# The first batch of a fused attention and FFN kernel: other first loads, scales written by ScalarE, and a new issue order

## The chip, the cores and the metric

The kernel runs on one core of a Trainium2 chip. The time is the device time of one execution in microseconds (us). A result is the median of several executions. Ratios are the mean time of one kernel's fast runs over that of the kernel before in the same rounds on the same chip, so they are not quite the ratio of the medians that are quoted beside them. A span is the length of one profiled execution; it is about 1.8 us shorter than that execution's time.

Engines: PE is TensorE (PEld its weight loads), DVE is VectorE, ACT is ScalarE, POOL is GpSimd, SP is SyncE. A name with a q (SPq, ACTq) is the engine's instruction queue, seen when it issues a DMA.

## The reference, cut to what matters

```python
# q, k, v: 8 batches x 8 heads x 576 rows x 64;  w_phi: 64 x 128
def phi(x):
    proj = einsum('bhsd,df->bhsf', x, w_phi)
    proj = proj - max(abs(proj), axis=-1, keepdims=True)
    return concatenate([exp(proj), exp(-proj)], axis=-1)
kv  = einsum('bhsf,bhsd->bhfd', phi(k), v);   z   = sum(phi(k), axis=2)
num = einsum('bhsf,bhfd->bhsd', phi(q), kv);  den = einsum('bhsf,bhf->bhs', phi(q), z) + 1e-6
x = (num / den) as 4608 rows x 512
out = (max(x @ w_gate, 0) * (x @ w_val)) @ w_out        # 512 -> 1536 -> 512
```

Each batch's x feeds the FFN. TensorE has most to do in the FFN, and that can't start before the first batch's attention has given its first x. The time until then is the ramp.

## The kernel before

All work is cut into some 850 pieces, and a list of numbers, `ORDER` ("the list" below), gives the order in which they are emitted. Every engine then runs its own instructions strictly in that order. A token `44:6` is piece 44 in PSUM bank 6 (or the pair 6 and 7); `z14:2` stands for 14 units of dummy matmul on zeros, which are meant to keep TensorE's clock up where the model expected it to be idle. The loads are pieces too: 1 is wv0 (a third of w_val), 2 wg0, 10 wg2 (the last third of w_gate), 12 wo0, 15 qm0 (tail rows of q, two small DMAs), 16 k2 (k of batch 2), 17 kt2 (tail rows of k, four small DMAs); 6 is wg1 and 13 wo1. A batch's tail is its last 64 rows of 576; late k is k of heads 4 to 7 of batch 0. A value scaling multiplies v by the scales (`scale_v` below), a kv product is a matmul of phi(k) with scaled v, an xu is the finished x of one chunk of 128 rows, and a k piece is k of two heads.

```python
def scale_v(dst, src, ek):                 # v times exp of the row maxima, on GpSimd
    nc.gpsimd.tensor_tensor(dst[:, :, :, 0:D], src ..., ek ..., op=ALU.mult)
    nc.gpsimd.tensor_copy(dst[:, :, :, D], ek)          # the scale itself, for z
# the row's normaliser: x = u * r, also on GpSimd, then transposed by TensorE to feed the FFN
    nc.gpsimd.tensor_tensor(x["xu"], x["u"][:, :, 0:D], r.to_broadcast([P, 8, D]), op=ALU.mult)
def k_crosswise(st):                       # groups 0 and 1 of batch 0: maxima and exps by half
    for par in range(2):
        k_max(st, 4, slice(par, par + 1)); k_exps(st, 4, 0, slice(1 - par, 2 - par))
    k_scales(st, 4)
# ... the first loads:
nc.scalar.dma_start(out=wf[0:D], in_=w_phi)
nc.gpsimd.dma_start(out=w2[D:P], in_=w_phi)
for u in range(NU):                        # NU = 4 groups of two heads
    if u < 2:
        load_kqv(0, "kn", k, nc.sync, FP32, slice(2 * u, 2 * u + 2))     # k piece u
    load_v(0, 2 * u, 2 * u + 2, nc.scalar)
load_first_tail(0); load_tail(inputs["vt", 0], 0, 1, v, nc.sync)
make_identity(nc, ident[FP32]); nc.gpsimd.tensor_copy(ident[BF16], ident[FP32])
for u in range(2):
    nc.gpsimd.dma_start(out=late_k[...], in_=k[0, 4 + 2 * u : 6 + 2 * u, 0:SF, :] ...)
# ...
nc.scalar.copy(w2[0:D], wf[0:D])           # the w copy: the first projection needs it
```

Of the kernel before, what the change touches and what calls it, by code (L numbers as in the profile page):

```python
# [46 lines left out]
ORDER = """z22:0 43:76 48:5 44:6 45 z6:4 49:0 z14:2 53:5 0 50 z12:4 54:2 65:7 3 59:6 4 56 1 5 z9:4 66:4 46 67  # L47
68 60:0 61 62 51 55 z56:7 70:4 77 69 84:5 52:6 63 71:02 72 7 11 73 47:7 z9:4 102:6 108:5 114:4 64:2
103:0 9 78:63 104 57 80 8 2 97:5 17 58:2 79 109:3 110 10 74:52 98:6 75:2 111 99 81:52 15 z15:3 76:4
105 82:3 126:2 120:5 85:03 87 139:2 100 86 533:7 88:53 121:0 525:2 6 83:7 89 90 541:2 122 16 526:7  # L50
13 115:3 527:5 101 106 152 123 107:2 18 170 116 117 91:67 168 112 124 528:5 542:7 171 92:6 113:0
94:51 95:2 535:7 543:6 127:30 129 536:7 118 12 128 544:2 177 130:50 96:7 93:3 131 534:4 119:2 125:7
140:53 14 132 142 529:2 133:70 539:1 162 134:4 136:32 537:0 141 538:7 530:1 545:0 189 137:7 20 546:4
21 143:52 153 144 163:0 145 531:7 547:4 164 135:2 19 552:3 166 165 138:5 172:6 173 540:2 553 149:45
554 167 169 150:0 146:12 183 175 174 548:5 549:4 532:3 154:60 155 550 156 147:5 551 221 184:2 22
190:0 178:6 555:5 556 558:4 186 179 180 229 191 185 557 559 187 151:6 192 148:7 157:23 176:5 560
561:3 158:76 195 196:40 197 567:2 24 583:3 181 193 188:6 198 208 159:7 182:4 23 223 241 160:5 562:0
199:61 200 242:3 201 194:5 243 563:0 25 26 584:1 568:2 244 28 575:7 230:5 224:0 222 565:2 573:3 231
225 205:47 566:2 574:3 235 226 232 564:7 206:4 577:2 260 202:30 245 273 576:1 579:7 203:2 227 580:0
236:5 289 209:31 238 211 204 578:7 233 585:0 210 569:1 237 570:2 591:7 291 207 29 212:53 213 239  # L60
581:1 214 571:2 33 298 572:3 215:45 582:6 228:1 246:2 247 30 218:35 240:1 219:4 592 216:2 234:1 283
220 593 292 248:53 284:1 249 217 586 587 310 250 304 588:7 251:35 285 290 252 594:0 595 253 589 286
27 254:65 596 257:34 255:5 590 597:6 598:4 258:7 603:5 287 305:0 342 307 256 261:26 31 263 613:4 262
161 306 609:5 604:6 316 308 614:7 615:4 299:0 264:26 265 266 610:5 605:4 356 300 34 601:6 302 301
274 602:7 35 616:5 259 270:62 32 309:3 617:4 267:75 271:0 618:1 607:6 272 608:2 599:7 311:0 329
275:35 313 277 600:2 611:7 276 312 288 619:5 303:6 606:2 394 620:7 268:0 612:1 293:2 317:46 295
624:0 318 627:1 269 628 319 294 625 320:62 321 357:4 412 410 314 629 626 343 322 296 358 278:23 344
297:6 279:71 350 315:0 39 280:3 639:6 359 323:20 630:1 37 360 637:3 326:07 324:6 631 345:4 351:2 38
347 632 362 352 621:0 327:7 622 635:6 623 281:1 325 633:7 346 634:6 638:0 353 419 354 640:1 330:46
331 653:0 332 645:1 348 654:2 36 646:3 355:0 333:16 363:4 334 335 636:3 647:0 643:6 413 42 364  # L70
339:73 328 644:2 411 365 649:6 361:3 648:7 366 340:0 336:12 655:6 651:7 425 337:0 381 395 349:5 341
652:6 396:13 426:5 397 641:7 398 427 656:0 663:4 642:7 368 428 367:3 650:2 414:0 369:52 664 666:7
338 416 463 667 41 431 370 665 371 689:2 668 420:5 515 422 415 372:03 374 373 421 657:2 660:7 450
661 691:3 669:4 378:56 423 375:01 376:3 662 658 379:4 40 659 687:1 404 399:03 670:2 690:1 405:6
382:42 407 477 417 384 683:0 671:1 429 406 383 692:2 688:3 408 400:01 681:2 684:3 672:1 675:2 385:64
432:0 386 673:3 424:2 387 433 434 682:4 418:5 377 388:36 465 679:7 674:2 464 677:4 391:30 437 389:1
380 676:2 685:7 680:0 471 430:1 435 392:7 686:6 409 390 393 678:5 483 478:3 480 438:60 693:2 694 439
699:5 440 436:0 695 484:6 479 282 441:30 481 700 702:2 442 443 701 485 696:0 486 705:1 703 401:3
447:45 444:67 697 402:1 704 445:3 698 709:7 706:4 707:5 472:6 451:02 474 453 708:4 452 516 710:5
719:2 473 448:3 482:4 713:5 723:0 454:61 466:3 502 456 489 455 724:5 720:0 446 717:1 467 711:2 714:5  # L80
457:01 460:67 449 468 475 469 712:2 715:5 458:1 487 461:0 718:3 470:4 727:7 490:15 491 716:4 732:0
725:7 492 733 488:1 721:2 476:1 493:35 462 459 494 728:7 729:2 726:1 722:7 403 730 495 738:1 496:73
731 745:4 497:3 498 499:56 747:2 743:7 734 500:6 503:24 735:7 741:0 736 504 739 740 505 737 506:52
742:4 746:7 744:0 507 508 748:1 509:45 510:0 749:6 751:7 750:3 759:2 760:1 512:07 513:6 752:5 757:4
753:7 761:6 755:0 758:7 756:1 517:24 518 519 768:0 763:1 501 511 771:7 754:6 762:5 764:4 769 774:3
514 520:21 775 521:65 522:4 765:1 772 776 770 777:2 799:6 766 781:0 767 773 779:0 778:6 800:7 780:5
523:6 787:4 782:7 788:3 793:2 783:1 784:0 794:7 524 797:6 789:5 791:7 798:6 785:0 792:7 813:1 790:0
786:2 795:1 804:0 801:7 796:6 802 805 806 810:1 807:2 803 811 823:0 812 817:3 808 809 829:7 814:6
818:5 824:7 815:6 816:0 827:7 819:1 828:0 835:2 830:1 821:0 836:7 831:6 820:5 822:7 833:6 834:0
825:7 826:1 832:0 837:2 838 846:3 839 847:7 843:6 848:7 840:5 841 844 845 842"""  # L90
# [6 lines left out]
def kernel(  # L97
# [23 lines left out]
    P = 128  # L121
# [127 lines left out]
    def scale_v(dst, src, ek):  # L249

        nc.gpsimd.tensor_tensor(  # L251
            dst[:, :, :, 0:D],
            src[:, :, None, :].to_broadcast([P, *dst.shape[1:3], D]),
            ek[:, :, :, None].to_broadcast([P, *dst.shape[1:3], D]),
            op=ALU.mult,
        )
        nc.gpsimd.tensor_copy(dst[:, :, :, D], ek)  # L257
# [15 lines left out]
    def k_exps(st, n, at, pars=slice(0, 2)):  # L273

        if "kp" not in st:
            st["kp"] = st["pool"].tile([P, 2, 2, 4, F], BF16, name="kp")
        kp = st["kp"][:, :, :, at : at + n]
        for s, sign in ((0, 1.0), (1, -1.0)):
            nc.scalar.activation(kp[:, s, pars], st["rows"][:, pars], AF.Exp, scale=sign)  # L279

    def k_max(st, n, pars=slice(0, 2)):

        if "m" not in st:
            st["m"] = sb_s.tile([P, 8], FP32, name="mk")[:, 0 : 2 * n]
        m = st["m"].rearrange("p (j i) -> p i j", i=2)
        row_max(m[:, pars], st["rows"][:, pars])

    def k_scales(st, n):
        st["ek"] = sb_s.tile([P, 8, 2], FP32, name="ek", bufs=8)[:, 0 : 2 * n]
        for s, sign in ((0, -1.0), (1, 1.0)):  # L290
            nc.scalar.activation(st["ek"][:, :, s], st["m"], AF.Exp, scale=sign)  # L291

    def k_crosswise(st):

        for par in range(2):
            k_max(st, 4, slice(par, par + 1))
            k_exps(st, 4, 0, slice(1 - par, 2 - par))
        k_scales(st, 4)

    def k_values(st, b, u):  # L300
        vs = st["vs"] = sb_k.tile([P, 8, 2, E], BF16, name="vs")
        vn = inputs["vn", b][:, 2 * u : 2 * u + 2].rearrange("p h c d -> p (h c) d")
        scale_v(vs, vn, st["ek"])

    def k_values_tail(st, b, at):

        ekm = sb_s.tile([P, NU, 2, 2], FP32, name="ekm", bufs=2)
        nc.gpsimd.tensor_tensor(
            ekm,
            st["ek"][:, at : at + NU, :, None].to_broadcast([P, NU, 2, 2]),  # L310
            half[:, None, None, :].to_broadcast([P, NU, 2, 2]),
            op=ALU.mult,
        )
# [3 lines left out]
    def k_kv(st, b, u, copy):  # L317
# [21 lines left out]
        copy(kv.rearrange("p h s e -> p (h s e)"), pk[:, 0 : 4 * E])  # L339
# [265 lines left out]
    def k_pieces(rank, st, start, ops, needs, take, name, banks, late=(), n=4, at=0, wide=True):  # L605
# [12 lines left out]
        if wide:  # L618
            wide_pieces(rank, st, n, at)
# [4 lines left out]
            lambda: k_crosswise(st),  # L624
            [
                ("DVE", 0.6),
                ("ACT", 0.48, None),
                ("ACT", 0.48, None),
                ("DVE", 0.6, 2),
                ("ACT", 0.48, 0),  # L630
                ("ACT", 0.48, 0),
                ("ACT", 0.21, 3),
            ],
            [(rank, "proj")],
            (rank, "rows", 0),
            free=[((rank, "proj"), 5)],
        )

    def wide_pieces(rank, st, n, at, done=lambda: None):
        plan.add(  # L640
            rank,
            "kmax",
            lambda: (k_max(st, n), k_scales(st, n)),
            [("DVE", 0.1 + n * 0.287), ("ACT", 0.21)],
            [(rank, "proj")],
            (rank, "rows", 0),
# [499 lines left out]
```

## Time and profile before

| | before |
|---|---|
| time, median | 390.13 us |
| span of the profiled execution | 388.2 us |
| TensorE busy | 374.4 us, of which dummy matmuls 11.9 us |
| TensorE without dummies | 362.5 us (374.4 - 11.9) |
| first FFN matmul | 34.1 us |
| last idle of TensorE in the ramp ends | 41.7 us |

The table by stretches of the kernel before. After the stretch and its length: busy time (and instructions) of PE, PEld, DVE, ACT and POOL, then TensorE's granted clock, the busy share of the DMA engines (transfers overlap, so it can exceed 1), and GB/s.

```profile
0.00:10.00 10.00, 5.88 (x32) 2.74 (x32) 2.42 (x9) 2.94 (x6) 6.38 (x14) 0.89 0.91 205
10.00:20.00 10.00, 9.92 (x100) 5.73 (x98) 7.60 (x12) 8.76 (x23) 7.83 (x8) 0.94 1.31 207
20.00:30.00 10.00, 7.50 (x136) 5.99 (x134) 9.58 (x18) 6.42 (x15) 8.93 (x13) 0.91 1.25 249
30.00:40.00 10.00, 9.15 (x138) 7.24 (x137) 7.26 (x14) 8.56 (x17) 7.85 (x11) 0.92 1.42 189
40.00:45.00 5.00, 4.15 (x96) 4.03 (x94) 3.75 (x6) 4.43 (x11) 5.00 (x5) 1.00 1.34 189
45.00:50.00 5.00, 5.00 (x101) 4.58 (x97) 4.39 (x11) 3.77 (x8) 3.68 (x5) 1.00 1.43 149
```

TensorE has gaps in the first 42 us and none from 45 us on; the DMA engines are full all the time. Parts of the timeline matter (start, length, engine, line, operation, out<-in; in brackets the idle time before it and what ended that). First the start, on all engines:

```profile
5.61 0.66 PE L240 MATMUL pall<-ident,vn 128*128 128x128 f32 x4 [0.90 <-DMA vn<-in_k_dram]
...
7.84 0.30 ACT L1036 CAST w<-wf 64x128 bf16<-64x128 f32 x1 [5.61 <-DMA kt<-in_k_dram]
8.19 0.61 PE L265 MATMUL pall<-w,tT 64*128 64x128 bf16 x8 [1.93 <-ACT w L1036]
...
11.19 1.91 POOL L251 TENSOR_TENSOR vs<-vn,ek 128x1024 bf16<-128x1024 f32 x1 [3.63 <-ACT ek L291]
```

The second k piece comes at 5.6 us. The first projection waits for the w copy on ScalarE at 7.84 us, and the first value scaling on GpSimd starts at 11.19 us. Then GpSimd around 35 us:

```profile
32.25 0.68 POOL L172 DMA_DIRECT2D qm<-in_q_dram  x1 [1.24 <-DMA wv_sb<-in_moe_w_val_dram]
...
34.79 0.82 POOL L215 DMA_DIRECT2D wg_sb<-in_moe_w_gate_dram  x1 [0.62 <-DMA kt<-in_k_dram]
35.61 0.90 POOL L163 DMA_DIRECT2D kn<-in_k_dram  x1
36.49 0.77 POOL L222 DMA_DIRECT2D wo_sb<-in_moe_w_out_dram  x1
37.26 0.25 POOL L308 TENSOR_TENSOR ekm<-ek,half 128x16 f32<-128x16 f32 x1
```

GpSimd issues loads one after the other: wg1, k2 and wo1 (in this list wg2 came earlier), some of them after a wait for an earlier DMA, and only then starts on the second batch's tail (37.26 us). TensorE, at the end of the ramp:

```profile
39.81 1.07 PE L457 MATMUL pall<-xT,wv_sb 128*128 128x128 bf16 x16
41.73 0.65 PE L323 MATMUL pall<-vs,kp 128*128 128x65 bf16 x16 [0.85 <-POOL vs L257]
```

It waits 0.85 us for the second batch's value scaling. That wait is the last in the ramp.

### The profile page before, as it was taken

To read this page: it belongs to the slowest core of one execution; us is meant where nothing else is said; L and a number is where in the kernel's file an instruction comes from. 1 tells how busy PE (TensorE), PEld (TensorE's weight loads), DVE (VectorE), ACT (ScalarE), POOL (GpSimd) and SP (SyncE) were. 2 spreads that over 40 slices of the span, in tenths; PEclk is the share of its full clock that TensorE was granted. 3 is DMA by queue.
4 is the path that set the end of the run, shared out by engine and by line. 5 is a ranking of instruction groups with operands and counts; after the bars stand their busy time and mean duration, and the time that the engine had idled before them with its cause. 6 is when DMAs were issued, how large, how long until landed. Compare 5 with 4: busy or idle time off the path is not lost.

```text
span 388.2 us, 8993 instructions
## 1 busy us (share of the span) xinstructions
PE 374.4 (96%) x3611; PEld 209.2 (54%) x3611; DVE 239.7 (62%) x413; ACT 240.2 (62%) x479; POOL 157.1 (40%) x178
## 2 busy tenths in 40 slices
PE   5979999999999999999999999999999999999994
PEld 2557898665465454645545465555545454444452
DVE  2797898868866777776746876577437443322330
ACT  2968868898848868778675767586463513413311
POOL 6797855684770684564305526236021101000000
PEclk9998999999999999999999999999999999999999
DMA  8999998999999794999474332210222011002003
GB/s 205 207 250 188 188 223 118 177 209 220 161 121 165 180 180 78 184 227 162 54 138 79 112 70 69 86 25 2 41 81 71 14 43 66 14 29 81 1 15 95
DMA packets 92506, 44.94 MB, mean 116 GB/s; under 512 B 58352, under 2 KB 87984, under 8 KB 92464
## 3 DMA queue, kind: packets, MB, share of 16 engines
q1 hardware_dynamic: 62352, 28.98, 33.5%
q0 software_dynamic: 28464, 13.78, 27.8%
q10 hardware_dynamic: 1648, 1.61, 1.3%
q8 instruction: 28, 0.46, 0.5%
q14 instruction: 14, 0.11, 0.1%
HBM read 37.81 MB, written 9.44 MB: 122 GB/s over the span
## 4 chain that ended last, share of the span: by engine, by line
PE 87%; POOL 6%; issue 3%; DMA 3%; DVE 0%; ACT 0%; ACTq 0%; POOLq 0%; DVEq 0%
PE pall L457 48%; PE pall L483 23%; PE pall L402 5%; PE pall L265 4%; PE pall L323 4%; DMA kt<-in_k_dram 3%; PE pall L357 2%; POOL vs L251 2%; PE pall L331 1%; POOL vsm L251 1%; PE pall L510 1%; POOL wv_sb L215 0%; POOL wg_sb L215 0%; PE pall L429 0%; DVE h L470 0%
## 5 line engine op out<-in xcount | busy, mean ns | idle before, releaser
L470 DVE SCALAR_TENSOR_TENSOR h<-pall,val_sb 128x512 bf16<-128x512 f32 x108 | 73.8, 686 | 74.9 <-PE pall L457 67.2
L466 ACT CAST val_sb<-pall 128x512 bf16<-128x512 f32 x108 | 63.5, 596 | 59.5 <-PE pall L457 47.5
L483 PE MATMUL pall<-wo_sb,h 128*128 128x512 bf16 x420 | 99.9, 379 | 0.0
L457 PE MATMUL pall<-xT,wv_sb 128*128 128x512 bf16 (+1 forms) x528 | 95.1, 321 | 0.5 <-ACT val_sb L466 0.5
L457 PE MATMUL pall<-xT,wg_sb 128*128 128x512 bf16 (+1 forms) x528 | 94.0, 321 | 0.0
L419 POOL TENSOR_TENSOR xu<-u,r 128x512 bf16<-128x512 f32 x36 | 37.4, 1044 | 124.8 <-DVE r L417 86.6
L251 POOL TENSOR_TENSOR vs<-vn,ek 128x1024 bf16<-128x1024 f32 x32 | 61.0, 1907 | 37.5 <-ACT ek L291 32.6
L279 ACT ACTIVATE kp<-pall 128x1024 bf16<-128x1024 f32 (+1 forms) x78 | 70.4, 966 | 8.5 <-PE pall L265 7.7
L457 PEld LDWEIGHTS <-wv_sb 128*128 128x128 bf16 x576 | 47.0, 98 | 41.7 <-issue 0.6
L457 PEld LDWEIGHTS <-wg_sb 128*128 128x128 bf16 x576 | 46.7, 98 | 40.1
L483 PEld LDWEIGHTS <-h 128*128 128x128 bf16 x420 | 38.6, 98 | 42.0
L247 DVE TENSOR_REDUCE mq<-pall 128x8 f32<-128x1024 f32 x36 | 43.8, 1220 | 17.2 <-PE pall L265 13.6
L247 DVE TENSOR_REDUCE mk<-pall 128x8 f32<-128x1024 f32 (+1 forms) x39 | 43.8, 1133 | 5.3 <-PE pall L265 3.2
L493 ACT COPY out_sb<-pall 128x512 f32<-128x512 f32 x35 | 20.5, 589 | 40.6 <-PE pall L483 37.5
L411 DVE TENSOR_TENSOR t<-pall,cq 128x455 f32<-128x455 f32 (+3 forms) x80 | 33.5, 419 | 17.8 <-PE pall L402 14.1
L374 ACT ACTIVATE qp<-pall 128x512 bf16<-128x512 f32 x60 | 36.6, 610 | 3.2 <-PE pall L357 3.1
L414 DVE TENSOR_TENSOR u<-pall,t 128x455 f32<-128x455 f32 (+3 forms) x80 | 34.2, 428 | 6.5
L375 ACT ACTIVATE qp<-pall 128x512 bf16<-128x512 f32 x60 | 37.0, 617 | 0.0
L402 PEld LDWEIGHTS <-qp 128*128 128x128 bf16 x640 | 27.5, 98 | 11.6 <-issue 1.2
L402 PE MATMUL pall<-kv,qp 128*128 128x65 bf16 x640 | 29.9, 195 | 1.2 <-DVE u L414 0.9
L323 PE MATMUL pall<-vs,kp 128*128 128x65 bf16 x512 | 20.7, 193 | 1.0 <-POOL vs L257 0.9
L323 PEld LDWEIGHTS <-kp 128*128 128x128 bf16 x512 | 18.8, 97 | 4.5 <-issue 1.3
(69 smaller groups left out, 269.2 us busy)
## 6 DMA issues: line engine op xcount, KB each, us to landing
out_dram<-out_sb SPq DMA_DIRECT2D x32, 256.0 KB, 2.4
vn<-in_v_dram SPq DMA_DIRECT2D x7, 1024.0 KB, 6.8
qn<-in_q_dram POOLq DMA_DIRECT2D x8, 512.0 KB, 8.2
kn<-in_k_dram POOLq DMA_DIRECT2D x7, 512.0 KB, 8.5
wv_sb<-in_moe_w_val_dram POOLq DMA_DIRECT2D x3, 512.0 KB, 13.3
wg_sb<-in_moe_w_gate_dram POOLq DMA_DIRECT2D x3, 512.0 KB, 10.3
wo_sb<-in_moe_w_out_dram POOLq DMA_DIRECT2D x3, 512.0 KB, 10.5
vn<-in_v_dram ACTq DMA_DIRECT2D x4, 256.0 KB, 5.6
```

The lines of the kernel that those rows point to most:

```text
L247: nc.vector.tensor_reduce(m, banks, axis=AX.X, op=ALU.max, apply_absolute_value=True)
L251: nc.gpsimd.tensor_tensor(dst[:, :, :, 0:D], src[:, :, None, :].to_broadcast([P, *dst.shape[1:3], D]), ek[:, :, :, None].to_broadcast([P, ...
L279: nc.scalar.activation(kp[:, s, pars], st["rows"][:, pars], AF.Exp, scale=sign)
L323: nc.tensor.matmul(kv_ps[:, hh, s, :], lhsT=st["kp"][:, s, c % 2, 2 * hh + c // 2], rhs=st["vs"][:, 4 * hh + c, s, :], start=(hh == s == c ...
L374: nc.scalar.activation(x["qp"][:, s, a], cols[:, 0], AF.Exp, scale=sign)
L375: nc.scalar.activation(y["qp"][:, s, b], cols[:, 1], AF.Exp, scale=sign)
L402: nc.tensor.matmul(banks[s][:, i], lhsT=x["qp"][:, s, slot, P * blk : P * (blk + 1)], rhs=kvs[b, h // 2][:, h % 2, s, :],)
L419: nc.gpsimd.tensor_tensor(x["xu"], x["u"][:, :, 0:D], r.to_broadcast([P, 8, D]), op=ALU.mult)
L457: nc.tensor.matmul(ps[:, n * i : n * (i + 1)], lhsT=w[:, dc, P * fi : P * fi + P], rhs=xT[:, dc, lo:hi], start=(dc == 0), stop=(dc == NDC ...
L466: nc.scalar.copy(st["val", step], ps)
L470: nc.vector.scalar_tensor_tensor(st["h2"][:, fis[0] : fis[-1] + 1, lo:hi], ps.rearrange("p (a b) -> p a b", b=n), 0.0, st["val", step].rea ...
L483: nc.tensor.matmul(st["po", t], lhsT=st["h2"][:, fi, P * t : P * t + P], rhs=wo_sb[:, fi, :], start=(fi == 0), stop=(fi == NFC - 1),)
```

## The change

Its intent: shorten the chain that leads to the first x. ScalarE writes the scales into v's extra column by itself, so that GpSimd copies nothing; groups 0 and 1 of batch 0 are handled at full width, with the two signs of exp as separate pieces; w is loaded in two halves on two queues and copied in one piece; late k goes first on GpSimd, in one DMA, and GpSimd's other loads are held until the second k piece is in; and the whole list is ordered anew after a model of the issue times. Cut to its core:

```diff
-    def k_crosswise(st): ...
+    if "z" in st:                                        # in k_scales, batch 0
+        vs = st["vs"] = sb_k.tile([P, 8, 2, E], BF16, name="vs")
+        for s, sign in ((0, -1.0), (1, 1.0)):
+            nc.scalar.activation(vs[:, :, s, D], st["m"], AF.Exp, scale=sign)
+    def k_scales_halves(st):                             # first tail: masked by a bias of -1e30
+        ... nc.scalar.activation(st["ekm"][:, :, s, hh], st["m"], AF.Exp, scale=sign, bias=other[...])
-        copy(kv..., pk[...])                             # batch 0: VectorE
+        nc.scalar.copy(kv..., pk[...])
-    nc.scalar.dma_start(out=wf[0:D], in_=w_phi)
-    nc.gpsimd.dma_start(out=w2[D:P], in_=w_phi)
+    nc.gpsimd.dma_start(out=late_k, in_=k[0, 4:8, 0:SF, :] ...)
+    for u, eng in enumerate((nc.scalar, nc.sync)):
+        if u:
+            eng.dma_start(out=wf[D * u : D * (u + 1)], in_=w_phi)
+        load_kqv(0, "kn", k, nc.sync, FP32, slice(2 * u, 2 * u + 2))
+        if not u:
+            eng.dma_start(out=wf[D * u : D * (u + 1)], in_=w_phi)
+    for lo, hi in ((0, 2), (2, 4), (4, 8)):
+        load_v(0, lo, hi, nc.scalar)
+    held = singles.tile([P, 1], FP32)
+    nc.gpsimd.tensor_copy(held, inputs["kn", 0][:, 2, 0, 0:1])
-    nc.scalar.copy(w2[0:D], wf[0:D])
+    nc.scalar.copy(w2, wf)
-ORDER = ... 143 dummy units ...
+ORDER = ... 92 dummy units; wv0 and wg0 behind the value scalings of batch 0 ...
```

## The prediction

> **What bounds the kernel now.** From about 42 us on TensorE never waits: the table by stretches shows it busy 50.0 of 50 us in nearly every stretch from 50 to 350 us. Only the ramp is open. Before 42 us TensorE is busy 33.6 us, of which 11.9 us (group of L999, 39 matmuls) are dummy matmuls on zeros; so useful work is 21.7 us and 20.3 us are lost. All that the change can win lies there: once the FFN matmuls run without gaps (first at 34.1 us, no gap after 41.7 us), each us saved before is one of the end.
>
> **The chain in the ramp (timeline, waits).** The first k transposes are in SBUF at 5.3 us, but the first projection starts at 8.19 us: it waits for the w copy on ScalarE (7.84 us), which stands in program order behind five DMA issues, the last of them held back until 7.43 us. The first row maxima are then interleaved with half-wide exps, and GpSimd's first value scaling starts at 11.19 us. From there GpSimd is the chain: scalings of 1.91 us, each with a 0.25 us copy of the scales, a 0.22 us mask product, DMA issues between; the last ends at 24.3 us, the first numerator at 26.2 us, the first FFN matmul at 34.1 us.
>
> **Removed.** One of ScalarE's DMA issues ahead of the w copy; GpSimd's w load; about 1.5 us of copies and mask on GpSimd; weight and k1 issues between the scalings. **Added.** Per group two ScalarE exps of about 0.16 us, four small ones for the first tail, kv evacuations on ScalarE (0.39 us) instead of VectorE (0.42 us); one GpSimd op that holds the q load until the second k piece is in. **Moved.** Half of w to the SyncE queue, late k first on GpSimd, wv0/wg0 behind all four scalings, w copy early.
>
> **Sum.** I estimate the w copy at 4.5 to 6 us, projection at about 5.5, first maximum (1.22 us) and scales by 8.1: first scaling 3 us earlier. Then 1.5 us less on GpSimd and fewer issues between: the last scaling of the first batch ends near 19.5 to 20 us instead of 24.3. Not all of the 4.5 us reaches the end: DMA is full from 2 us to 60 us (slices), and wv0, issued near 20 us instead of 6 us, takes about 10 us to land (issue table: 13.3 us median), so the FFN starts near 29.5 to 31 us. The Trainium skill ("DMA: Bandwidth & Descriptors", section "Issuing engines are not separate DMA queues") says that all issuers share 16 engines, so using both queues saves issue time, not transfer time; the trace agrees (9 tenths busy while three queues run). As a second count, the dummy units in the order fall from 143 to 92; at 11.9/143 = 0.083 us that is 4.3 us, if the order's model is right. I take 3.7 us.
>
> **Prediction.** 386.5 us, range 383.3 to 389.6. Faster by over 2%: 0.06; within 2%: 0.92; slower: 0.02.
>
> **What would show it.** w copy before 6 us; first scaling near 8; last of the first batch near 20; first FFN matmul near 30; dummy matmuls near 7.7 us; useful TensorE work unchanged (362.5 us); stretches after 50 us unchanged.
>
> **What would make it wrong.** The w copy still held behind the larger last v issue (gain under 2 us); wv0 or wg0 landing late (FFN waits on DMA); the first k pieces slowed by the late k load now issued first; new gaps in mid-kernel from the reordered list.

## The result

The changed kernel takes 395.26 us at the median (four fast runs, 393.79 to 396.44) against 390.13 us. The ratio is 1.013, with an interval of 1.0092 to 1.0169. It is 1.3% slower, clear of the noise and outside the predicted range.

| | before | after |
|---|---|---|
| span | 388.2 us | 392.8 us |
| TensorE busy without dummies | 362.5 us | 375.5 - 8.6 = 366.9 us |
| dummy matmuls | 11.9 us | 8.6 us |
| w copy | 7.84 us | 5.06 us |
| first value scaling | 11.19 us | 8.83 us |
| last value scaling of batch 0 ends | 24.3 us | 22.3 us |
| first FFN matmul | 34.1 us | 32.8 us |
| second batch's tail scaling begins | 37.3 us | 45.2 us |

The table by stretches, of the changed kernel:

```profile
0.00:10.00 10.00, 6.82 (x36) 3.59 (x36) 3.29 (x12) 3.20 (x8) 4.17 (x11) 0.93 0.85 208
10.00:20.00 10.00, 6.45 (x76) 4.75 (x74) 5.90 (x9) 8.77 (x25) 7.72 (x7) 0.67 1.29 200
20.00:30.00 10.00, 8.99 (x125) 5.85 (x123) 7.02 (x12) 8.00 (x16) 7.09 (x9) 0.89 1.02 209
30.00:40.00 10.00, 9.83 (x170) 8.42 (x169) 9.04 (x20) 8.60 (x17) 6.58 (x9) 1.00 1.30 205
40.00:45.00 5.00, 0.55 (x6) 0.50 (x6) 1.32 (x2) 0.91 (x5) 2.50 (x3) 0.78 1.58 170
45.00:50.00 5.00, 5.00 (x60) 4.61 (x58) 2.94 (x4) 2.54 (x5) 4.86 (x7) 0.54 1.34 176
```

Up to 40 us TensorE's busy time is about level with before (32.1 against 32.5 us, dummies included). From 40 to 45 us TensorE works 0.55 us of 5, and from 45 to 50 us its granted clock is 0.54. TensorE's timeline there:

```profile
38.99 1.06 PE L468 MATMUL pall<-xT,wg_sb 128*128 128x128 bf16 x16
44.50 0.61 PE L440 MATMUL pall<-ident,xu 128*128 128x128 bf16 x4 [4.45 <-POOL xu L430]
44.91 1.91 PE L468 MATMUL pall<-xT,wg_sb 128*128 128x128 bf16 x16
...
49.94 1.06 PE L468 MATMUL pall<-xT,wg_sb 128*128 128x128 bf16 x16
```

It stood 4.45 us for an xu of GpSimd. Sixteen FFN matmuls then took 1.91 us where they take 1.06 us before and after. The Trainium skill ("TensorE: Matmul & The Clock Gate", section "What's actually happening") says that the array runs at half clock after an idle window of about 3.4 us; this trace agrees, with 0.54 granted after 4.45 us of idle. GpSimd's timeline says why the xu was late:

```profile
26.12 0.79 POOL L216 DMA_DIRECT2D wg_sb<-in_moe_w_gate_dram  x1
...
34.90 1.06 POOL L430 TENSOR_TENSOR xu<-u,r 128x512 bf16<-128x512 f32 x1
36.81 0.74 POOL L173 DMA_DIRECT2D qm<-in_q_dram  x1 [0.85 <-DMA qn<-in_q_dram]
39.30 0.68 POOL L173 DMA_DIRECT2D qm<-in_q_dram  x1 [1.75 <-DMA wv_sb<-in_moe_w_val_dram]
42.47 0.90 POOL L164 DMA_DIRECT2D kn<-in_k_dram  x1 [2.49 <-DMA wg_sb<-in_moe_w_gate_dram]
43.39 1.05 POOL L430 TENSOR_TENSOR xu<-u,r 128x512 bf16<-128x512 f32 x1
44.38 0.82 POOL L223 DMA_DIRECT2D wo_sb<-in_moe_w_out_dram  x1
45.23 0.23 POOL L319 TENSOR_TENSOR ekm<-ek,half 128x16 f32<-128x16 f32 x1
```

The xu at 43.39 us stands behind the issue of k2, and that issue waited until 42.47 us for wg2, which was issued at 26.12 us. (wg2's landing was 15.8 us after its issue, the longest of the three w_gate loads in the view of that tile.) The start, on all engines, in the changed kernel:

```profile
5.06 0.30 ACT L1041 CAST w<-wf 128x128 bf16<-128x128 f32 x1 [2.83 <-DMA wf<-in_w_phi_dram]
...
5.41 0.40 PE L267 MATMUL pall<-w,tT 64*128 64x128 bf16 x8
...
7.76 0.66 PE L241 MATMUL pall<-ident,vn 128*128 128x128 f32 x4 [1.95 <-DMA vn<-in_k_dram]
7.77 0.19 POOL L1040 COPY held<-vn 128x1 f32<-128x1 f32 x1 [4.63 <-DMA vn<-in_k_dram]
...
8.83 1.92 POOL L252 TENSOR_TENSOR vs<-vn,ek 128x1024 bf16<-128x1024 f32 x1
...
16.88 1.06 PE L334 MATMUL pall<-vs,kp 128*128 128x65 bf16 x16 [3.55 <-ACT kp L281]
```

The w copy came as early as predicted, and the first value scaling too. But the second k piece, which its transposes need, came at 7.76 us and not at 5.6 us, and GpSimd was held for it as well. The first kv product at 16.88 us waited 3.55 us for ScalarE's exps.

### Why an issue waits for a landing

The listing of GpSimd's program names the semaphores that each instruction waits for. Below are the DMAs of the changed kernel, counted by hand in issue order; what each one waits for among GpSimd's own DMAs is the program's.

```
#0 late k    #1 q0    #2 k1    #3 wv1    #4 wv0    #5 wg0    #6 wg1
#7  q1       waits DMASW1 (its buffer: q0)
#8  wv2      waits DMASW0          (#0)
#9  wg2      (none named)
#10 kt2 a    waits DMASW2 (#2)     #11 kt2 b   waits DMASW3 (#3)
#12 kt2 c    waits DMASW4 (#4)     #13 kt2 d   waits DMASW5 (#5)
#14 wo1      waits DMASW6 (#6)
   xu (another chunk)
#15 qm0 a    waits DMASW7 (#7)     #16 qm0 b   waits DMASW0 (#8: wv2)
#17 k2       waits DMASW1 (#9: wg2), and TensorE
   xu (chunk 1)                    <- what TensorE stood for
#18 wo0      waits DMASW2 (#10)
   second batch: tail scaling, value scalings
```

Eight semaphores are used in turn, so every DMA of GpSimd waits, in program order, until the one issued eight before it has landed, and everything behind it on GpSimd waits too. The six small loads (kt2, qm0) each use up one of the eight. In the kernel before, k2 is issued directly behind wg1, and what stands eight before it is a small kt2 load, which had landed at 34.74 us; k2 was issued at 35.61 us without a wait. (The wait of 0.62 us ahead of wg1 there is of the same kind: by that program's listing wg1 waits for the DMA eight before it, wg0.) The queues of SyncE and ScalarE share a like set of eight (DMAHW0 to 7): in the kernel before the fourth v load is issued at 7.43 us after such a wait, and the w copy stood behind it.

### The profile page after: what moved, and what is told of

It is laid out like the page before. It is cut to its first block, busy times and chain, and to the rows that moved or that the text cites. A ratio compares the mean times of both kernels' runs of the same rounds, so it can differ in the third digit from the quotient of the medians.

```text
span 392.8 us, 8947 instructions
## 1 busy us (share of the span) xinstructions
PE 375.5 (96%) x3598; PEld 211.2 (54%) x3598; DVE 239.3 (61%) x410; ACT 242.7 (62%) x489; POOL 155.7 (40%) x172
## 4 chain that ended last, share of the span: by engine, by line
PE 85%; DMA 6%; POOL 4%; issue 3%; SPq 1%; ACT 0%; POOLq 0%
PE pall L468 47%; PE pall L494 22%; PE pall L413 4%; DMA wg_sb<-in_moe_w_gate_dram 4%; PE pall L267 4%; PE pall L334 3%; PE pall L368 2%; DMA xT<-xu 2%; POOL vs L252 2%; PE pall L342 1%; PE pall L521 1%; POOL wv_sb L216 1%; POOL qn L164 0%; PE pall L440 0%; POOL wg_sb L216 0%
## 5 line engine op out<-in xcount | busy, mean ns | idle before, releaser
L468 PE MATMUL pall<-xT,wv_sb 128*128 128x512 bf16 (+1 forms) x528 | 96.1, 323 | 0.5 <-DMA xT<-xu 0.5
L468 PE MATMUL pall<-xT,wg_sb 128*128 128x512 bf16 (+1 forms) x528 | 95.9, 324 | 0.0
L468 PEld LDWEIGHTS <-wg_sb 128*128 128x128 bf16 x576 | 47.9, 99 | 40.1
L385 ACT ACTIVATE qp<-pall 128x512 bf16<-128x512 f32 x60 | 36.5, 608 | 7.0 <-PE pall L368 7.0
L413 PE MATMUL pall<-kv,qp 128*128 128x65 bf16 x640 | 30.7, 194 | 0.0
L334 PE MATMUL pall<-vs,kp 128*128 128x65 bf16 x512 | 21.5, 196 | 3.6 <-ACT kp L281 3.6
L334 PEld LDWEIGHTS <-kp 128*128 128x128 bf16 x512 | 19.5, 100 | 7.4 <-ACT kp L281 3.7
## 6 DMA issues: line engine op xcount, KB each, us to landing
wg_sb<-in_moe_w_gate_dram POOLq DMA_DIRECT2D x3, 512.0 KB, 10.1
```

The costliest lines, as they stand in the source:

```text
L334: nc.tensor.matmul(kv_ps[:, hh, s, :], lhsT=st["kp"][:, s, c % 2, 2 * hh + c // 2], rhs=st["vs"][:, 4 * hh + c, s, :], start=(hh == s == c ...
L385: nc.scalar.activation(x["qp"][:, s, a], cols[:, 0], AF.Exp, scale=sign)
L413: nc.tensor.matmul(banks[s][:, i], lhsT=x["qp"][:, s, slot, P * blk : P * (blk + 1)], rhs=kvs[b, h // 2][:, h % 2, s, :],)
L468: nc.tensor.matmul(ps[:, n * i : n * (i + 1)], lhsT=w[:, dc, P * fi : P * fi + P], rhs=xT[:, dc, lo:hi], start=(dc == 0), stop=(dc == NDC ...
```

## The experiments

Theory A: the time is lost at this hole, because GpSimd stands at a load's issue with TensorE's input behind it. Theory B: it is lost earlier, by the late second k piece and what follows from it. All kernels gave correct results. The times, with the first FFN matmul of the profiled run:

| run | median us | ratio to before (interval) | first FFN matmul |
|---|---|---|---|
| after | 395.26 | 1.0130 (1.0092 to 1.0169) | 32.8 |
| e1_xu_first | 391.34 | 1.0039 (1.0003 to 1.0076) | 32.4 |
| e2_loads_late | 391.09 | 1.0025 (0.9980 to 1.0070) | 37.0 |
| e3_new_parts_old_order | 393.98 | 1.0094 (1.0064 to 1.0125) | 39.6 |
| e4_old_parts_new_order | 395.10 | 1.0123 (1.0098 to 1.0147) | 36.5 |
| e5_k_before_w | 392.05 | 1.0042 (1.0023 to 1.0062) | 34.0 |
| e6_late_k_later | 391.60 | 1.0021 (0.9992 to 1.0051) | 36.2 |
| e7_both | 390.53 | 1.0010 (0.9989 to 1.0031) | 34.3 |
| e8_zeros_in_holes | 395.47 | 1.0132 (1.0111 to 1.0152) | 37.0 |
| e9_k1_on_act | 388.66 | 0.9970 (0.9938 to 1.0003) | 31.7 |
| e10_wv0_earlier | 393.13 | 1.0063 (1.0034 to 1.0093) | 32.0 |
| e11_k1_act_wv0 | 388.55 | 0.9960 (0.9941 to 0.9979) | 30.9 |
| e12_before_w_first | 392.26 | 1.0042 (1.0009 to 1.0074) | 32.5 |
| e13_before_w_and_loads | 387.76 | 0.9921 (0.9885 to 0.9957) | 31.8 |
| e14_before_loads_late | 389.54 | 0.9963 (0.9930 to 0.9996) | 34.6 |
| e15_best_q_first | 389.62 | 0.9950 (0.9896 to 1.0003) | 34.5 |
| e16_tail_loads_moved | 393.55 | 1.0079 (1.0036 to 1.0122) | 35.9 |

The runs of one kernel differ by more than the usual 0.3% in many rows (e2: 389.81 to 393.50). The landing of the first loads, which differs from run to run, is a likely reason, but that was not tested. The rounds ran on several chips, so runs of different rounds are best compared by their ratios; differences of medians below are rounded pointers. The profiled run of e2 is its slowest (393.50 us) and that of e12 its fastest (390.09 us), so the last column is one draw for each kernel.

### e1 and e2: the loads out of the way

In both, only load tokens of the changed kernel's list move.

```diff
 e1: ... 101:1 531:5 87:02
-    15 539:3 127:4 114:1 129 16 z3:2 102:2 111 88:3 12 ...
+    539:3 127:4 114:1 129 z3:2 102:2 111 88:3 15 16 12 ...
 e2:
-    15 ... 16 ... 88:3 12 ... 122 124 ...
+    ... 88:3 ... 122 124 15 16 12 ...
```

> The changed kernel, with only the qm0 and k2 loads moved behind the x scaling (xu) of chunk 1 in GpSimd's program. Theory A (the loss is GpSimd standing in front of a DMA issue that waits for a DMA issued eight before, wg2, to land at 41.9 us, with the xu that TensorE needs behind it): the idle of TensorE at 40.1 to 44.5 us and the half clock after it shrink, but GpSimd then stands at the same loads before the second batch's tail scaling, so I expect a part, 390 to 392 us. Theory B (the loss lies before 30 us, in the late second k piece and the cold clock there): no change, 395 us.

> As the last, but qm0, k2 and wo0 moved behind all four value scalings of the second batch. Theory A: GpSimd meets no landing before it has done what TensorE needs; the hole is gone and none comes in its place: 387.5 to 389.5 us. Theory B: 395 us.

e1 took 391.34 us and e2 391.09 us: some 4 us less than the changed kernel, where theory B expected nothing. e1 lies in its range, e2 a little above its own. In e1 the idle times of TensorE that are left in 36 to 50 us are the first and the last line here; the line between them, without a wait, is where the hole was:

```profile
36.10 0.40 PE L442 MATMUL pall<-ident,xu 128*128 128x128 bf16 x4 [0.47 <-POOL xu L432]
...
39.97 0.39 PE L442 MATMUL pall<-ident,xu 128*128 128x128 bf16 x4
...
48.48 0.65 PE L336 MATMUL pall<-vs,kp 128*128 128x65 bf16 x16 [1.66 <-POOL vs L261]
```

The 4.45 us are gone (the 0.47 us are of the chunk before). A wait of 1.66 us for the second batch's scaling took its place, because GpSimd met wg2's landing just after. In e2 neither is there, but a new wait comes later: the five issues of qm0, k2, wo0 and another third of w_out keep GpSimd from 53.98 to 57.81 us with an xu behind them, and TensorE waits 1.32 us for it at 58.93 us. So "none comes in its place" was wrong. Theory A holds for the hole. But e2 is still not faster than the kernel before, with 4.6 us to the predicted 386.5 us: something else is lost as well.

### e3 and e4: the parts and the list, each alone

e3 has every edit of the change, with the old list (renumbered; a split piece stands as several in its place). e4 is the kernel before with the new list.

> All of the change except the order list: the list of before, its pieces renumbered (a piece that is now several stands as several in its place). If the order list is at fault (theory A): no hole at 40 us, the parts alone are worth 1 to 3 us: 387 to 389.5 us. If the parts are at fault (late k first, w halves on the queues, GpSimd held): 392 to 396 us.

> The kernel before with the new order list (a split piece stands where its first part stood). Theory A: the hole is there, 394 to 398 us, as the loads of GpSimd stand in the new order. If the parts are at fault: 389 to 391 us.

Both are slow: 393.98 and 395.10 us. For e3 I was wrong: the parts alone, in the old list, cost time as well. In its profile the second k piece landed only at 9.74 us; the old list puts that piece's transposes ahead of the first projection, which then came at 10.79 us, and the first FFN matmul at 39.6 us instead of 34.1 us. So part of theory B is true too. The new list makes the other part: in e4's profile GpSimd issued k2 only at 43.51 us, again after a wait (2.23 us) for wg2, with the xu behind it at 44.42 us, and TensorE waited 1.94 us for that xu. The hole goes with the list, and e4 is as slow as the whole change (1.0123 against 1.0130).

### e5, e6, e7: the second k piece

Counted in the trace, the packets of 1 KB of the two k pieces end, in the kernel before, by 4.0 us but for a dozen stragglers (500 of 512), the last at about 5.0 us. In the changed kernel the 500th ends at 6.9 us. Packets that ended in each half microsecond from 4.5 to 7 us of the changed kernel:

```
second k piece (SyncE, 1 KB)   27   52   56   62   44
v (ScalarE, 1 KB)              53   47   54   55   64
late k (GpSimd, 512 B)         62   76   57   54   60
```

In these counts three queues share the engines in about equal numbers of packets (not of bytes: those of late k are half as large). The Trainium skill ("DMA: Bandwidth & Descriptors", section "Queues, rings and completion order") says that each DMA engine goes round the queues that have work, packet by packet; these counts agree from 5 us on. In the kernel before, the same packets ended at 119 to 154 per half microsecond from 2.5 to 4 us, with hardly anything beside them. Putting half of w ahead of the second k piece let ScalarE's v in first, and late k came as a third. The edits, on e2:

```diff
 e5, e7:
-        if u:
-            eng.dma_start(out=wf[D * u : D * (u + 1)], in_=w_phi)
         load_kqv(0, "kn", k, nc.sync, FP32, slice(2 * u, 2 * u + 2))
-        if not u:
-            eng.dma_start(out=wf[D * u : D * (u + 1)], in_=w_phi)
+        eng.dma_start(out=wf[D * u : D * (u + 1)], in_=w_phi)
 e6, e7: the late-k DMA after the copy of the identity instead of first
```

> The version with the loads late (qm0, k2, wo0 behind the second batch's scalings), and in the SyncE queue the second k piece issued before the second half of w, not after it. Seen so far: the last packet of the second k piece ends at 5.0 us in the kernel before and at 7.0 to 9.3 us with the changed loads. Theory C (it comes late because the w load put ahead of it lets a v load of ScalarE slip in front): the piece is in by about 5 us and the time falls to 387.5 to 389.5 us. If the early late-k load of GpSimd is what holds it up: still 7 us or later, 390 to 392 us.

> The version with the loads late, and GpSimd's late-k load issued after the identity (about 3 us) as in the kernel before, the w half still ahead of the second k piece. If the late-k load issued first takes the second k piece's share of the DMA engines: the piece is in by 5.5 us, 387.5 to 389.5 us. If the w load is what holds it up: 6.5 us or later, 390 to 392 us.

> Both of these edits on the version with the loads late. Theory C and its rival agree: the second k piece in by 5 us, scalings of the first batch start near 8 us and follow without the gap at 12.4 us, end near 19 us; 386 to 388.5 us, and less spread between runs.

In e5 the last packet of the second k piece ends at 4.1 us, in e6 at 8.1 us, in e7 at 5.6 us. So, by one trace of each, the order of w and the second k piece decides, and late k adds little (8.1 against 8.9 us in e2). But the time did not follow: 392.05, 391.60 and 390.53 us. In e5 and e7 the w copy came only at 7.89 and 8.16 us, because the second half of w was now the late one. One early input was bought with another late one, and the first FFN matmul stayed at 34.0 to 36.2 us.

### e8: dummy matmuls in the holes

```diff
-  ... 49:2 ... 89:0 ...
+  ... z40:2 49:2 ... z70:0 89:0 ...
```

> The changed kernel with dummy matmuls added where TensorE stood idle: 40 units before the first kv product (idle 13.3 to 16.9 us) and 70 before the x transposes of chunk 1 (idle 40.1 to 44.5 us). The waits stay; only the clock is kept up. Useful TensorE work took 366.9 us in the changed kernel against 362.5 us before. If the cold clock after the holes is the loss that stays: 391 to 392.5 us; if the waits alone are (the work after them would have waited anyway): 394 to 396 us.

The time stayed, 395.47 us. As a test of the time it missed its aim. The first set of dummies writes PSUM bank 2 and waited itself, until 18.65 us, so it came after the hole and not in it, and took 4.42 us there. The second set ran from 43.89 to 47.83 us, although the xu was there by 45.6 us:

```profile
47.67 0.39 PE L442 MATMUL pall<-ident,xu 128*128 128x128 bf16 x4
```

The two traces still size the clock's part. From these transposes to the end of the span, the same instructions take 393.7 - 47.67 = 346.0 us in e8, where the granted clock is 1.00 from 40 to 55 us, and 392.8 - 44.50 = 348.3 us in the changed kernel, where it is 0.54 from 45 to 50 us; in neither does TensorE wait more than 0.6 us at a time after that point. So I estimate the half clock behind the hole at 2.3 us, from one trace each. e8 began this stretch 3.2 us later and won 2.3 us in it, so the total hardly moved. The run tells something else as well: its first FFN matmul came at 37.0 us, 4.2 us later than in the changed kernel (32.8 us), and the total is the same. While the hole is there, the start doesn't set the end.

### e9 and e11: both inputs early

On e2: the first k piece goes on SyncE and the second on ScalarE, then the halves of w on both, then v; late k after the identity; and the w copy ahead of the last v issue. e11 also has the load of wv0 right behind that of wv1.

```diff
+    for u, eng in enumerate((nc.sync, nc.scalar)):
+        load_kqv(0, "kn", k, eng, FP32, slice(2 * u, 2 * u + 2))
+    for u, eng in enumerate((nc.sync, nc.scalar)):
+        eng.dma_start(out=wf[D * u : D * (u + 1)], in_=w_phi)
+    for lo, hi in ((0, 2), (2, 4)):
+        load_v(0, lo, hi, nc.scalar)
     ...
     nc.scalar.copy(w2, wf)
+    load_v(0, 4, 8, nc.scalar)
 e11, in the list too:  4 1 ... -> wv0 (1) moved directly behind wv1 (5)
```

> The version with the loads late, and the first issues rearranged: the first k piece on SyncE, the second on ScalarE, then the two halves of w, then v; late k after the identity; the w copy ahead of the last v issue. The two last runs mended the second k piece only to have the w copy at 7.9 to 8.2 us. Theory C2 (the start pays only when both are early: then ScalarE does not stand between 8.5 and 10.9 us before the second group's exps, and the first kv product does not wait 3.5 us for ScalarE): w copy and second k piece by 5.5 us, first kv product before 16 us, 386 to 388.5 us. Rival (the start is not what the end waits for, weights landing are): 390 to 391.5 us as before.

> The rearranged first issues, the loads late, and wv0 early. If both the start and the landing of the weights bind: the best of all, 385.5 to 388 us. If neither: 390 us.

388.66 us and 388.55 us. By the ratios e9 is some 2 us below e2, but their intervals overlap a little (0.9938 to 1.0003, 0.9980 to 1.0070); that of e11 (0.9941 to 0.9979) lies below those of e2 and e7 and below 1, so e11 beats the kernel before. In e11 GpSimd's hold ended at 4.43 us, the w copy came at 5.29 us and the first FFN matmul at 30.9 us, as the prediction had it. e9's w copy was later than expected, 6.28 us. So the start does pay once the hole is gone. That w and the second k piece must both be early fits e5 to e7, which had one of them each; but e9 and e11 differ from e7 also in the queues and the place of the w copy, so it isn't shown alone. The first kv product still waited 3.53 us for ScalarE in both, where I had expected that wait to go. That wv0 comes earlier added nothing here that the medians can show. A wait of the same kind was left in the start. The last v issue now stood ahead of the first scales on ScalarE:

```profile
7.86 0.38 ACTq L166 DMA_DIRECT2D vn<-in_v_dram  x1
8.28 0.31 ACT L295 ACTIVATE ek<-mk 128x8 f32<-128x8 f32 x2 [2.70 <-DVE tT L246]
```

By the listing this issue waits for a tail load of k (it landed at 7.84 us), while the maxima behind the scales were ready at 7.36 us. So e11's first value scaling began at 8.68 us, hardly earlier than the changed kernel's 8.83 us. And as in e2, the late issues held an xu (1.12 us at 53.67 us).

### e10: is it wg2's landing?

The changed kernel, with nothing but wv0's load moved from behind the four scalings of the first batch (22.2 us) to directly behind wv1's.

> The changed kernel with one token moved: the load of wv0 issued right after that of wv1, before the value scalings of the first batch instead of behind them (22.2 us). In the changed kernel the DMA engines stood at 0.64 and 0.91 of their time from 22 to 26 us, and wg2 landed at 41.9 us, which is what GpSimd waited for. Theory A says the hole ends when wg2 lands, so it shrinks by what wg2 lands earlier, 2 to 3 us: 392 to 393.5 us. If the scalings, 0.8 us later, count more: 395 us or more.

It took 393.13 us, 2.1 us less. GpSimd's timeline:

```profile
40.35 0.90 POOL L166 DMA_DIRECT2D kn<-in_k_dram  x1 [2.07 <-DMA wg_sb<-in_moe_w_gate_dram]
41.27 1.05 POOL L432 TENSOR_TENSOR xu<-u,r 128x512 bf16<-128x512 f32 x1
```

k2 was issued at 40.35 us instead of 42.47 us, also 2.1 us earlier, and TensorE's wait for the xu shrank from 4.45 to 3.33 us. The medians differ by as much as the issue did (the profiled runs by 1.6 us). In the changed kernel, e4 and e10 the x transposes start 2.0 us after the issue of k2 (42.47 and 44.50 us, 43.51 and 45.53, 40.35 and 42.38), while their first FFN matmuls lie from 32.0 to 36.5 us.

### e12, e13, e14: does it hold in the old order?

The kernel before, with one edit each, and with both.

```diff
 e12, e13:
-        load_v(0, 2 * u, 2 * u + 2, nc.scalar)            # four issues, then the w copy
+        if u < 2: load_v(0, 2 * u, 2 * u + 2, nc.scalar)
     nc.scalar.copy(w2[0:D], wf[0:D])
+    for u in range(2, NU): load_v(0, 2 * u, 2 * u + 2, nc.scalar)
 e13, e14, in the list: qm0, k2 and their transposes (15, 16, 152, 168) behind 124,
     three of the second batch's four value scalings
```

> The kernel before with one edit: the w copy stands ahead of the third and fourth v issue on ScalarE, not behind them. The prediction took the 7.84 us of the w copy as the start of the chain. If so: projection at about 5.6 us, first scaling 2 to 2.5 us earlier, 387.5 to 389 us. If the chain is set elsewhere (weights landing, second batch): 389.5 to 390.5 us.

> The kernel before with the w copy ahead of the last two v issues and, new, qm0 and k2 (with their transposes) behind three of the second batch's four scalings. If the pinned DMA issues swallow the early gain: the second batch's tail scaling starts near 34.5 us instead of 37.3 us and the time is 387.5 to 389 us. If the early gain is lost elsewhere: 390 to 392 us.

> The kernel before with only that move of qm0 and k2, the w copy late as before. Pinning theory: GpSimd reaches the tail scaling 1 to 2 us earlier, but its inputs and the x of the first batch come no earlier: 389 to 390.3 us, so that both edits together give more than the sum of each. Otherwise 390 to 392 us.

e12 gained nothing (392.26 us; 390.09 us in its profiled run). There the w copy came at 4.00 us, the first FFN matmul at 32.5 us, 1.6 us earlier than before, and yet GpSimd's timeline is this:

```profile
34.88 0.82 POOL L215 DMA_DIRECT2D wg_sb<-in_moe_w_gate_dram  x1 [0.79 <-DMA kt<-in_k_dram]
...
37.34 0.25 POOL L308 TENSOR_TENSOR ekm<-ek,half 128x16 f32<-128x16 f32 x1
```

These are the 34.79 and 37.26 us of the kernel before, within 0.1 us. TensorE:

```profile
41.82 0.64 PE L323 MATMUL pall<-vs,kp 128*128 128x65 bf16 x16 [2.53 <-POOL vs L257]
```

It now waits 2.53 us where it waited 0.85 us. What the start had won, 1.6 us, it stood there: 2.53 - 0.85 = 1.7 us. That explains the profiled run, which is even with the kernel before. Why the other three runs of e12 are 2 us slower than that, no profile shows. With qm0 and k2 out of the way as well (e13), GpSimd comes to the second batch at 33.40 us:

```profile
30.86 1.04 POOL L421 TENSOR_TENSOR xu<-u,r 128x512 bf16<-128x512 f32 x1 [2.77 <-DVE r L419]
31.84 0.81 POOL L217 DMA_DIRECT2D wg_sb<-in_moe_w_gate_dram  x1
32.64 0.76 POOL L224 DMA_DIRECT2D wo_sb<-in_moe_w_out_dram  x1
33.40 0.25 POOL L310 TENSOR_TENSOR ekm<-ek,half 128x16 f32<-128x16 f32 x1
```

No wait for a DMA is left among these, TensorE has no idle time in 36 to 50 us, and the kernel takes 387.76 us, ratio 0.9921. That is the lowest median, and the kernel is faster than both the kernel before and the changed one. The move of the loads alone (e14) gives 389.54 us. In ratios, e12 has +0.4%, e14 -0.4%, and both together -0.8%: here the early start is worth something only where the loads don't pin GpSimd, that is hold it until a DMA lands. (e13 and e14 ran in the same rounds on one chip, and all runs of e13 lie below all of e14.)

### e16 and e15

e16 is the changed kernel with the four small kt2 loads (token 17) moved behind wo0. k2 stays ahead of the xu, but what stands eight before it is then wg0 and no longer wg2.

> The changed kernel with one token moved: the four small tail loads (kt2) go behind k2 and wo0, so that the DMA eight before k2 is wg0 and no longer wg2; k2 still stands ahead of the x scaling. If the hole is this eight-before wait: k2 is issued before 36 us, the x scaling is not held up, and the hole at 40 us is gone; GpSimd then meets wg2's landing at the tail loads, before the second batch's scalings, so I expect a smaller hole there, 390 to 393 us. If it is the full DMA queue as such that holds k2: the hole stays, 395 us.

```profile
38.75 1.43 POOL L175 DMA_DIRECT2D qm<-in_q_dram  x2
40.16 0.91 POOL L166 DMA_DIRECT2D kn<-in_k_dram  x1
41.08 1.06 POOL L432 TENSOR_TENSOR xu<-u,r 128x512 bf16<-128x512 f32 x1
```

k2 and the loads before it are issued without a wait, the xu follows at once, and TensorE has no hole at 40 us. wg2 landed only at 43.3 us (15.6 us after its issue), so k2 went out 3.1 us before the landing that it waited for in the changed kernel. The time is 393.55 us, a little above my range (its interval overlaps that of the changed kernel, so a gain in time isn't shown), and this profiled run had started late (first kv product at 18.45 us), so k2 was issued at 40.16 us and not before 36 us as I had written. Later it met a wait at the moved loads (1.38 us, for wo1 and not wg2), and TensorE waited 1.58 us for the second batch's scaling at 51.2 us. So it is the DMA eight before that holds the issue, and not a full queue as such.

e15 is e11 with the two q transposes (76, 90) ahead of the first kv product, to fill the 3.5 us there.

> The best version so far (first k pieces on two queues, loads late, wv0 early) with the two q transposes issued ahead of the first kv product, where TensorE stands 3.5 us for the tail's exps on ScalarE. If that wait costs what it holds up: the transposes and their VectorE copies are done in it and 0.5 to 1.5 us are won, 387 to 388.2 us. If the next steps wait for ScalarE all the same: 388.5 us.

389.62 us (387.12 to 392.28): nothing gained that can be told from the spread. In the profiled run, the slowest, the transposes themselves waited 3.72 us for ScalarE's exps, until 17.02 us. Their first PSUM bank (3) is, by the list, one of the pair that the tail's projection holds (2 and 3) until its exps are done, which is what the kv product waits for as well. That this bank is the reason was read from the list and not tested.

## Why the prediction was wrong

- "All that the change can win lies there: once the FFN matmuls run without gaps [...] each us saved before is one of the end." This step failed. The FFN matmuls ran from 32.8 us on, 1.3 us earlier, but not without gaps: GpSimd's issue of k2 waited for wg2 to land and held an xu, 4.45 us of idle time for TensorE, and then half clock (some 2.3 us more, estimated above). The prediction's own danger "new gaps in mid-kernel from the reordered list" is near to this, but it was neither placed at 40 us nor traced to an issue; and the same kind of wait stood in its own words, "the last of them held back until 7.43 us". Moving load tokens alone gave back 4 us (e1, e2), and in the old order a start 1.6 us earlier was swallowed whole (e12), until the loads were moved (e13).
- "the last scaling of the first batch ends near 19.5 to 20 us" was mis-sized: 22.3 us. In part this is the second k piece, which landed near 7.8 us instead of 5.6 us in the kernel before. I had named "the first k pieces slowed by the late k load" as a danger; it was the w half ahead of the piece that decided (e5 against e2 and e6). But with this piece and w both early (e11) the last scaling still ended at 21.3 us, so some 1.3 us of the miss have another cause; GpSimd's second scaling waited for ScalarE there.
- "the FFN starts near 29.5 to 31 us" was 32.8 us. In e11, with both inputs early, it was 30.9 us.
- "I estimate the w copy at 4.5 to 6 us" and "first scaling 3 us earlier" were right: 5.06 us, and 8.83 against 11.19 us, so 2.4 us.
- "wv0 or wg0 landing late (FFN waits on DMA)" came close and was not it: TensorE waited for no weights. GpSimd waited for wg2, in order to issue something else. That moving wv0 behind the scalings made the landing late is true all the same: moved back, 2.1 us were won (e10).
- "dummy matmuls near 7.7 us" were 8.6 us. As a count of gained time that number is worthless: the model behind the list doesn't include the wait of a load's issue for a landing. "useful TensorE work unchanged (362.5 us)": it measured 366.9 us. More matmuls ran at half clock: the granted clock was 0.67 from 10 to 20 us and 0.54 from 45 to 50 us, against 0.94 and 1.00 before. Of the second of these stretches 2.3 us are estimated above; the part of the first is open.
- The rest stays open. e11 with 388.55 us is 2 us above the prediction. The wait of some 3.5 us for ScalarE stands in every version with the new list, ahead of the first kv product or of what was put before it, and the late issues still cost e11 1.12 us.

## What to carry to other kernels

When an engine both computes and issues loads, ask of each load what has to land before it may be issued, and what stands behind it in the same program: a load needed later can hold up a result needed at once, so put it behind that result, and then look at what the moved issues hold up in their new place. Before pricing a faster start, look for the next point that is pinned to a DMA's landing; a microsecond won ahead of it shows only when that point moves too. And when first loads are rearranged, check that every early input of the first matmul is early, since here the queues shared the engines packet by packet, and one input's gain was another's delay (e5, e7).

## What the Trainium skill lacked or had wrong

- "DMA: Bandwidth & Descriptors", section "Why a DMA increments its semaphore by 16 and not by 1", asks for one semaphore per slot in flight. It doesn't say what reuse of the slots costs an in-order engine: with eight in turn, an issue stood up to 2.49 us for a landing (k2 for wg2), with an idle time of 4.45 us on TensorE behind it.
- The same page, section "Issuing engines are not separate DMA queues", says that issuing from several engines only saves the time of issuing. In these runs the order of issue over the two hardware queues also decided what landed when: the second k piece's last packet ended at 4.1 us or at 8.9 us (e5, e2) with one small w load after or before it, as the turns between queues that another section of the page describes would have it. The section alone lets a reader think that the choice of queue cannot matter.
- The same page, section "Anatomy of one DMA — SWDGE (gpsimd) path", fits one load as 2.0 us plus bytes over 436 GB/s. For the 1 MB (in memory) of a third of w_gate an estimate from this is 4.4 us (the page's own table of single transfers lies above its fit); with the queues full the three took 7.5, 10.1 and 15.8 us to land in the changed kernel. The page has no figure for the time from issue to landing with other loads queued ahead.
